# Split buffers two and two, result rows first on ScalarE, and the first gathers one by one: a change to a Fourier-and-experts kernel

## The chip, the cores and the metric

The kernel runs on one core of a Trainium2 chip. The metric is device time in microseconds, the median of several runs; one further execution was profiled.

## The reference, cut to what matters

The input `x` has 8 sequences of 1856 rows of 256 numbers. The reference takes the real part of its two-dimensional Fourier transform, and sends each of the 14,848 rows through one of 16 experts:

```python
X = np.fft.fft(x, axis=1); x = np.fft.fft(X, axis=2).real.reshape(B * S, D)
g_idx = argmax(x @ w_group)            # one of 4 groups
e_idx = argmax(x_g @ w_expert[g])      # one of 4 experts in it
h = maximum(x_e @ w1[g, e], 0)         # 256 -> 1024
ye = h @ w2[g, e]                      # 1024 -> 256
out[tokens] = (g_w * e_w)[:, None] * ye   # two softmax weights
```

## The kernel before, in words

**First phase.** `phase1` computes the transform batch by batch as matmuls in pairs of fp16 halves (a number is a high half plus a low half), chooses an expert for each row, and writes the rows of 260 words with their token number and weight to the DRAM tensor `XS`. The order of its steps is written out by hand, as the letters of `ORDER0` to `ORDER8`. Its last part, `last_rows`, is left over as a "tail" that the second phase runs between its own steps.

**Second phase.** `phase2` works through 44 jobs. A slot is 128 rows of one expert, and a job is one to four slots. The jobs are: 0, 1 and 2, the first four slots of experts 0, 1 and 2, taken before all batches are routed (kind "e"); 3, 4 and 5, three more slots of each (kind "s"); 6 and 7, four and three slots of expert 3; 8, one overflow slot (kind "o", whose expert is read from a table at run time); 9 and 10, expert 4; 11, overflow; and so on to expert 15. Overflow slots take the rows of experts that have more than seven slots.

For each slot POOL gathers 128 rows from `XS` by an indirect DMA (`gather`, L1243) into one of eight `xg` buffers. `turn_steps` casts the high half on ScalarE (L1263) into `xh`, of which there are four, makes the low half on VectorE (L1265), and a transposing DMA on SP's queue (L1271) writes `xT`. `layer1` makes eight groups of six matmuls (`ph`, L1301), each followed by a relu on ScalarE (L1304) and the low half on VectorE (L1305). `layer2` makes 24 matmuls a slot (`py`, L1317), ScalarE scales the result into one of four `y` buffers (L1322), and POOL stores it to `out` with an indirect DMA (L941). PSUM has four banks for `ph` and two for `py`.

**Weights.** A unit is the weights of one expert, 2 MB. `load_weights` (L1189) brings them into a staging buffer `wst`; `split_steps` squares them on ScalarE (`junk`), adds the sums across partitions with a tiny matmul on PE (`pn`, L1211), derives a power of two on VectorE, and writes the high half on ScalarE and the low half on VectorE into a split buffer `whl`. Before the change there is a staging `w` for experts' own weights, one for overflow weights (`wo`), three split buffers for own weights (`wa`, `w2`, `wx`, used in turn) and one for overflow weights (in `wo`). The list `todo` holds the units in the order in which their split buffers come free; `weights` makes one step of the first unit on it when that unit's buffer is free, and starts the next load into the same staging when a split ends. `begun` lets own units beyond the first three wait for job 3 and overflow units for job 4.

**Order.** While job n runs, its iteration starts the gathers of job n+2 (`fetch`, `serve`: all of a job's slots at once), emits `layer1` of job n, `layer2` of job n-1, and between the pieces (`tick`) steps of the weights' split, of the tail, and of the turning of job n+1 (`prep`). A piece of layer 1 counts 320 a slot and a piece of layer 2 counts 2570 of planned time, and a weights step is made for each 800 (1000 during the tail). This is the order in which the program is written down; the framework's scheduler then orders each engine's queue, by that order as priority and by planned times, except where `InOrder` (the names `self.A`, `self.V`, ...) pins an instruction behind those written down before it on its engine. The first two jobs' gathers, casts and transposes are emitted in the first phase, by `first_turn`: all eight gathers, then the casts.

```python
return "w", ("wa", "w2", "wx")[e % 3]     # pools(u): staging, split buffer
```

Of the kernel before, what the change touches and what calls it, by code (L numbers as in the profile page):

```python
# [49 lines left out]
STEADY = 8  # L50

# [252 lines left out]
class K:  # L304
# [780 lines left out]
    def early_load(self, e, r):  # L1085

        b, ii, ge = self.early[e, r]
        return self.gather(self.xp2, ii, b), ge
# [151 lines left out]
    def gather(self, pool, ap, b=None):  # L1240

        xg = pool.tile([P, RWID], F32, name="xg")
        ins = self.nc.gpsimd.indirect_dma_start(  # L1243
            out=xg[:, :].bitcast(I32), out_offset=None, in_=self.XS[:, :],
            in_offset=bass.IndirectOffsetOnAxis(ap=ap, axis=0),
            bounds_check=B * BSTEP, oob_is_err=False).ins
        if b is not None:
            self.of_batch(ins, b)
        return xg

    def turn_steps(self, qp, xgs, ges, V, A, Q, most=4, bufs=(3, 4)):
# [9 lines left out]
        for j, xg in enumerate(xgs):  # L1261
            xh = qp.tile([P, 2, D], F16, name="xh", bufs=bufs[1])
            A.copy(xh[:, 0], xg[:, 0:D])  # L1263
# [14 lines left out]
    def first_turn(self):  # L1278

        jobs = [[(e, r) for r in range(a, z)] for e, a, z in waves()[0][1]]  # L1280
        while jobs[-1][-1] not in self.early:
            yield
        xs = [list(zip(*(self.early_load(*j) for j in job))) for job in jobs]
        yield
        self.x0 = []
        most = max(map(len, jobs))
        for xgs, ges in xs:
            self.x0.append((yield from self.turn_steps(self.xp0, xgs, ges, self.V, self.A, self.Q, most,
                                                       (len(jobs), most))))
# [20 lines left out]
    def layer2(self, qp, w, hT, cws, toks, group="out"):  # L1310
        nc = self.nc
        for j, (cw, tok) in enumerate(zip(cws, toks)):
# [9 lines left out]
            nc.scalar.activation(y, py, AF.Copy, scale=cw)  # L1322
# [17 lines left out]
    def phase2(self, wp):  # L1340
        tc, nc = self.tc, self.nc
        wpa = self.wpa
        with tc.tile_pool(name="h", bufs=2, reuse_waits="tile") as hp, \
# [26 lines left out]
            def pools(u):  # L1370
                kind, e = units[u]
                if kind == "o":
                    return "wo", "wo"
                return "w", ("wa", "w2", "wx")[e % 3]
# [11 lines left out]
            state = dict(split=None, done=-1, t=0, tail=self.last_rows(), job=0)  # L1386
            begun = lambda u: u < len(first) or state["job"] >= LATER + (units[u][0] == "o")

            def tail():
                if state["tail"]:  # L1390
                    try:
                        next(state["tail"])
                    except StopIteration:
                        state["tail"] = None
                        pool["wo"] = later.enter_context(
                            tc.tile_pool(name="wo", bufs=1, side="right", reuse_waits="tile"))
                    serve()
# [13 lines left out]
            def weights():  # L1411

                if state["split"] is None:
                    if not todo or free(todo[0]) > state["done"] or (units[todo[0]][0] == "o" and "o" not in infos) \
                            or not begun(todo[0]):
# [14 lines left out]
            def fetch(n):  # L1430
                if n < len(jobs):
                    want.append(n)
                    serve()

            def serve():
                while want:
                    n = want[0]
                    _, kind, slots = jobs[n]
                    if state["tail"] and (kind != "e" or any(j not in self.early for j in slots)):
                        return  # L1440
                    want.pop(0)
                    if kind == "e":
                        if n >= len(self.x0):
                            xs[n] = list(zip(*(self.early_load(*j) for j in slots)))
# [3 lines left out]
                    if kind == "o" and "o" not in infos:  # L1448
                        infos["o"] = self.overflow_info(pool["wo"])
                    ii, ge = infos[kind]  # L1450
                    xs[n] = ([self.gather(self.xp2, ii[:, j:j + 1]) for j in slots],
                             [ge[:, j:j + 1] for j in slots])

            def prep(n):
                if n < len(jobs):
                    while n in want:
                        tail()
                    xs[n] = self.x0[n] if n < len(self.x0) else \
# [3 lines left out]
            def tick(g, t):  # L1462
                if t == T1 and state["job"] >= STEADY:
# [114 lines left out]
```

## Time and profile before

| | us |
|---|---|
| median of 3 runs | 861.6 |
| runs | 860.82, 861.6, 865.37 |
| profiled execution | 868.83 |
| its span, first to last instruction | 867.0 |

The span has 17,751 instructions. The mean granted TensorE clock over it is 0.991 of full speed. The first phase fills about the first 185 us; the first matmul of the expert layers is at 185.5 us. In the rows below, "busy" is time in which an engine executes, a wait is put down to what released it last, and SPq, POOLq and so on are the queues' own instructions, such as the issue of a DMA. PE is TensorE's matmuls, PEld its weight loads, ACT ScalarE, DVE VectorE, POOL GpSimd.

### The profile page before, as it was taken

To read this page: it belongs to the slowest core of one execution; us is meant where nothing else is said; L and a number is where in the kernel's file an instruction comes from. 1 tells how busy PE (TensorE), PEld (TensorE's weight loads), DVE (VectorE), ACT (ScalarE), POOL (GpSimd) and SP (SyncE) were. 2 spreads that over 40 slices of the span, in tenths; PEclk is the share of its full clock that TensorE was granted. 3 is DMA by queue.
4 is the path that set the end of the run, shared out by engine and by line. 5 is a ranking of instruction groups with operands and counts; after the bars stand their busy time and mean duration, and the time that the engine had idled before them with its cause. 6 is when DMAs were issued, how large, how long until landed. Compare 5 with 4: busy or idle time off the path is not lost. (4 is left out here: it accounts for less than half of the span.)

```text
span 867.0 us, 17751 instructions
## 1 busy us (share of the span) xinstructions
PE 815.2 (94%) x6491; PEld 585.2 (67%) x6491; DVE 550.6 (64%) x1381; ACT 581.1 (67%) x1190; POOL 318.7 (37%) x326
## 2 busy tenths in 40 slices
PE   1899999989889998999999999999999989999996
PEld 0467666656557776686868686868686858686865
DVE  6469998789863755474756566665656556654440
ACT  2477676876645876686777778686868677865531
POOL 1023211413674415253535262526262626240302
PEclk9999999999999999999999999999999999999998
DMA  9677973385686546565657574858485757443201
GB/s 348 192 223 202 248 219 136 141 233 214 143 192 200 161 147 195 127 175 160 177 167 199 132 225 106 218 126 242 94 226 114 225 105 226 119 139 64 63 5 42
DMA packets 105515, 144.53 MB, mean 167 GB/s; under 512 B 75194, under 2 KB 77638, under 8 KB 103888
## 3 DMA queue, kind: packets, MB, share of 16 engines
q1 hardware_dynamic: 91360, 106.15, 41.1%
q0 software_dynamic: 13632, 36.99, 18.2%
q8 instruction: 52, 0.85, 0.4%
q14 instruction: 39, 0.32, 0.1%
q10 hardware_dynamic: 432, 0.22, 0.1%
HBM read 97.41 MB, written 31.72 MB: 149 GB/s over the span
## 5 line engine op out<-in xcount | busy, mean ns | idle before, releaser
L1301 PE MATMUL ph<-xT,whl 128*128 128x512 f16 (+2 forms) x2112 | 353.9, 317 | 7.7 <-DVE hT L1305 5.0
L1317 PE MATMUL py<-whl,hT 128*128 128x256 f16 x2976 | 356.8, 272 | 4.2 <-ACT y L1322 4.2
L1317 PEld LDWEIGHTS <-hT 128*128 128x128 f16 x2976 | 287.2, 98 | 60.5 <-issue 7.6
L1305 DVE SCALAR_TENSOR_TENSOR hT<-ph,hT 128x512 f16<-128x512 f32 (+2 forms) x352 | 178.0, 529 | 156.6 <-ACT hT L1304 152.9
L1301 PEld LDWEIGHTS <-whl 128*128 128x128 f16 x2112 | 184.1, 98 | 128.2 <-issue 8.1
L941 POOL DMA_INDIRECT out<-y,tok x124 | 142.6, 1150 | 262.7 <-ACT y L1322 214.2
L1304 ACT ACTIVATE hT<-ph 128x512 f16<-128x512 f32 (+2 forms) x352 | 156.1, 471 | 50.4 <-PE ph L1301 45.4
L1243 POOL DMA_INDIRECT xg<-XS,ii_s x100 | 116.0, 1160 | 133.3 <-ACT hT L1304 83.8
L282 DVE SCALAR_TENSOR_TENSOR whl<-wst,e_v,whl 128x1024 f16<-128x1024 f32 x112 | 140.0, 1281 | 26.1 <-ACT whl L282 24.8
L282 ACT ACTIVATE whl<-wst,e_v 128x1024 f16<-128x1024 f32 x112 | 123.8, 1139 | 24.1 <-DVE e_v L282 21.4
L282 ACT ACTIVATE junk<-wst 128x1024 bf16<-128x1024 f32 x112 | 118.4, 1057 | 12.2 <-DMA wst<-w 11.8
L1322 ACT ACTIVATE y<-py,cws 128x256 f32<-128x256 f32 x124 | 58.3, 472 | 55.7 <-PE py L1317 39.2
L1263 ACT CAST xh<-xg 128x256 f16<-128x256 f32 x112 | 43.2, 403 | 70.8 <-DMA xT<-xh 64.1
L1265 DVE TENSOR_TENSOR xh<-xg,xh 128x256 f16<-128x256 f32 x112 | 46.6, 419 | 66.4 <-ACT xh L1263 66.3
L282 PE MATMUL pu<-CS,ghl 128*128 128x464 f16 (+3 forms) x384 | 81.9, 364 | 3.5 <-ACT ghl L282 3.5
L282 PEld LDWEIGHTS <-ghl 128*128 128x128 f16 (+1 forms) x384 | 43.7, 118 | 32.8 <-ACT ghl L282 3.5
L282 PEld LDWEIGHTS <-U 128*128 128x128 f16 x672 | 44.4, 99 | 14.4 <-issue 3.5
L282 PE MATMUL pr<-c,U 128*128 128x256 f16 x336 | 48.9, 283 | 3.5 <-DMA U<-un 2.2
L282 ACT CAST U<-pu 128x464 f16<-128x464 f32 (+3 forms) x64 | 32.7, 549 | 17.2 <-PE pu L282 16.2
L282 POOL DMA_DIRECT2D xq<-xq x12 | 11.0, 1072 | 85.4 <-DVE xq L282 26.5
L282 DVE TENSOR_TENSOR xq<-xq 128x514 f32<-128x514 f32 x40 | 25.4, 687 | 6.4 <-DMA xq<-xq 6.4
L282 DVE SCALAR_TENSOR_TENSOR ghl<-BD,x_v,ghl 128x512 f16<-128x512 f32 (+1 forms) x30 | 21.8, 781 | 2.1 <-ACT ghl L282 2.1
(183 smaller groups left out, 462.4 us busy)
## 6 DMA issues: line engine op xcount, KB each, us to landing
wst<-w SPq DMA_DIRECT2D x108, 512.0 KB, 8.2
xq<-xq SPq DMA_DIRECT2D x8, 1028.0 KB
xq<-xq POOLq DMA_DIRECT2D x12, 514.0 KB, 5.7
XS<-whl SPq DMA_DIRECT2D x6, 910.0 KB
CS<-cs SPq DMA_DIRECT2D x8, 464.5 KB, 10.2
XS<-row SPq DMA_DIRECT2D x3, 1040.0 KB
XS<-row SPq DMA_DIRECT2D x3, 910.0 KB
XS<-xq SPq DMA_DIRECT2D x3, 910.0 KB
```

The costliest lines, as they stand in the source:

```text
L282: return self.tc.keep_in_program_order(f(*args, **kw))
L941: ins = self.nc.gpsimd.indirect_dma_start(out=out, out_offset=bass.IndirectOffsetOnAxis(ap=ap, axis=0), in_=in_, in_offset=None, bounds_ch ...
L1243: ins = self.nc.gpsimd.indirect_dma_start(out=xg[:, :].bitcast(I32), out_offset=None, in_=self.XS[:, :], in_offset=bass.IndirectOffsetOnAx ...
L1263: A.copy(xh[:, 0], xg[:, 0:D])
L1265: lo = V.tensor_tensor(out=xh[:, 1], in0=xg[:, 0:D], in1=xh[:, 0], op=ALU.subtract)
L1301: nc.tensor.matmul(ph[:, 0:n * P], lhsT=w[:, wl, o:o + P], rhs=xT[:, xl * 2 + c, :], start=i == 0, stop=i == 5)
L1304: self.relu = nc.scalar.activation(hT[:, f, 0], ph[:, 0:n * P], AF.Relu).ins.name
L1305: nc.vector.scalar_tensor_tensor(out=hT[:, f, 1], in0=ph[:, 0:n * P], scalar=0.0, in1=hT[:, f, 0], op0=ALU.max, op1=ALU.subtract)
L1317: nc.tensor.matmul(py, lhsT=hT[:, f, hl, j * P:(j + 1) * P], rhs=w[:, wl, 2048 + f * D:2048 + (f + 1) * D], start=i == 0, stop=i == 23)
L1322: nc.scalar.activation(y, py, AF.Copy, scale=cw)
```

## The change

It has three parts.

- **Split buffers.** Own weights of the experts from 3 on use two split buffers in turn (`wo`, `w2`), overflow weights two others (`wa`, `wx`). The first three experts keep `wa`, `w2` and `wx`. The staging buffers stay as they were.
- **Result rows.** The activation that scales `py` into `y` is given a priority 400 places ahead of its place.
- **Gathers.** While the job number is under 8, the gathers of job n+2 are handed out one at a time, at every second piece of layer 1 of job n, each with a wait for the relu just emitted. From job 8 on they go out all at once as before. When the tail ends, what is then due goes out at once, behind the last relu emitted. In `first_turn` job 1's gathers come behind the first cast of job 0, with a wait for it.

```diff
--- before.py
+++ after.py
@@ -48,6 +48,7 @@
 LATER = 3
 OVER_AT = 4
 STEADY = 8
+URGENT = 400
 
 RATE, RATE2, T1, T2 = 1000, 800, 320, 2570
 
@@ -1082,10 +1083,10 @@
                                  in1=self.carry[:, e:e + 1].broadcast_to([P, r1 - r0]), op=ALU.is_ge)
         self.V.tensor_tensor(out=self.carry, in0=self.carry, in1=self.c32[:, o:o + NE], op=ALU.max)
 
-    def early_load(self, e, r):
+    def early_load(self, e, r, after=None):
 
         b, ii, ge = self.early[e, r]
-        return self.gather(self.xp2, ii, b), ge
+        return self.gather(self.xp2, ii, b, after), ge
 
     def of_batch(self, ins, b):
 
@@ -1237,7 +1238,7 @@
         self.w0 = yield from self.split_steps(self.wpa, self.st0, self.V, self.A, self.M,
                                               self.misc[:, 488:490])
 
-    def gather(self, pool, ap, b=None):
+    def gather(self, pool, ap, b=None, after=None):
 
         xg = pool.tile([P, RWID], F32, name="xg")
         ins = self.nc.gpsimd.indirect_dma_start(
@@ -1246,7 +1247,14 @@
             bounds_check=B * BSTEP, oob_is_err=False).ins
         if b is not None:
             self.of_batch(ins, b)
+        if after:
+            self.behind(ins, after)
         return xg
+
+    def behind(self, ins, name):
+
+        self.tc.add_manual_dep(ins, name, mybir.DependencyInfo(
+            mybir.DependencyClass.Sync, mybir.DependencyReason.DATA), reason="not before it")
 
     def turn_steps(self, qp, xgs, ges, V, A, Q, most=4, bufs=(3, 4)):
 
@@ -1260,7 +1268,7 @@
         xT = xT[:, :, 0:n * P]
         for j, xg in enumerate(xgs):
             xh = qp.tile([P, 2, D], F16, name="xh", bufs=bufs[1])
-            A.copy(xh[:, 0], xg[:, 0:D])
+            self.cast = A.copy(xh[:, 0], xg[:, 0:D]).ins.name
             yield
             lo = V.tensor_tensor(out=xh[:, 1], in0=xg[:, 0:D], in1=xh[:, 0], op=ALU.subtract)
             tw = V.scalar_tensor_tensor(out=wt[:, j], in0=ges[j].broadcast_to([P, 2]), scalar=BIG,
@@ -1280,13 +1288,18 @@
         jobs = [[(e, r) for r in range(a, z)] for e, a, z in waves()[0][1]]
         while jobs[-1][-1] not in self.early:
             yield
-        xs = [list(zip(*(self.early_load(*j) for j in job))) for job in jobs]
+        load = lambda job, after=None: list(zip(*(self.early_load(*j, after) for j in job)))
+        xs = load(jobs[0])
         yield
         self.x0 = []
         most = max(map(len, jobs))
-        for xgs, ges in xs:
-            self.x0.append((yield from self.turn_steps(self.xp0, xgs, ges, self.V, self.A, self.Q, most,
-                                                       (len(jobs), most))))
+        for i in range(len(jobs)):
+            steps = self.turn_steps(self.xp0, *xs, self.V, self.A, self.Q, most, (len(jobs), most))
+            next(steps)
+            if i + 1 < len(jobs):
+                xs = load(jobs[i + 1], self.cast)
+            yield
+            self.x0.append((yield from steps))
 
     def layer1(self, qp, w, xT, n):
         nc = self.nc
@@ -1319,7 +1332,8 @@
                                      start=i == 0, stop=i == 23)
                     i += 1
             y = qp.tile([P, D], F32, name="y", bufs=4)
-            nc.scalar.activation(y, py, AF.Copy, scale=cw)
+            with self.tc.high_priority(URGENT):
+                nc.scalar.activation(y, py, AF.Copy, scale=cw)
             if group is None:
                 nc.gpsimd.indirect_dma_start(
                     out=self.ap["out"], out_offset=bass.IndirectOffsetOnAxis(ap=tok, axis=0),
@@ -1370,8 +1384,8 @@
             def pools(u):
                 kind, e = units[u]
                 if kind == "o":
-                    return "wo", "wo"
-                return "w", ("wa", "w2", "wx")[e % 3]
+                    return "wo", ("wa", "wx")[e % 2]
+                return "w", ("wa", "w2", "wx")[e] if e < len(first) else ("wo", "w2")[(e - len(first)) % 2]
 
             pool = {"w": wp, "wa": wpa, "w2": wp2, "wx": wpx}
             last, before = {}, {}
@@ -1383,7 +1397,7 @@
             todo = sorted(range(1, len(units)), key=lambda u: (max(free(u), 0), u))
             st, ready, infos, xs, want = {}, {0: self.w0}, {}, {}, []
             self.scratch = wpx.tile([P, 2, 4096], F16, name="whl").rearrange("p h n -> p (h n)")
-            state = dict(split=None, done=-1, t=0, tail=self.last_rows(), job=0)
+            state = dict(split=None, done=-1, t=0, tail=self.last_rows(), job=0, turn=False)
             begun = lambda u: u < len(first) or state["job"] >= LATER + (units[u][0] == "o")
 
             def tail():
@@ -1394,7 +1408,7 @@
                         state["tail"] = None
                         pool["wo"] = later.enter_context(
                             tc.tile_pool(name="wo", bufs=1, side="right", reuse_waits="tile"))
-                    serve()
+                    serve(len(want))
 
             def load(u):
                 kind, e = units[u]
@@ -1412,7 +1426,7 @@
 
                 if state["split"] is None:
                     if not todo or free(todo[0]) > state["done"] or (units[todo[0]][0] == "o" and "o" not in infos) \
-                            or not begun(todo[0]):
+                            or not begun(todo[0]) or pools(todo[0])[1] not in pool:
                         return False
                     loads()
                     pn = self.ps.tile([P, 2], F32, name="pn", tag="r" if state["tail"] else "misc")
@@ -1428,38 +1442,45 @@
                 return True
 
             def fetch(n):
-                if n < len(jobs):
-                    want.append(n)
-                    serve()
-
-            def serve():
-                while want:
-                    n = want[0]
-                    _, kind, slots = jobs[n]
-                    if state["tail"] and (kind != "e" or any(j not in self.early for j in slots)):
+                if len(self.x0) <= n < len(jobs):
+                    xs[n] = []
+                    want.extend((n, j) for j in jobs[n][2])
+                    if state["job"] >= STEADY:
+                        serve(len(want))
+
+            def serve(most):
+                while want and most:
+                    n, j = want[0]
+                    kind = jobs[n][1]
+                    if state["tail"] and (kind != "e" or any(i not in self.early for i in jobs[n][2])):
                         return
                     want.pop(0)
+                    most -= 1
                     if kind == "e":
-                        if n >= len(self.x0):
-                            xs[n] = list(zip(*(self.early_load(*j) for j in slots)))
+                        xs[n].append(self.early_load(*j))
                         continue
                     if not infos:
                         infos["s"] = self.static_info()
                     if kind == "o" and "o" not in infos:
                         infos["o"] = self.overflow_info(pool["wo"])
                     ii, ge = infos[kind]
-                    xs[n] = ([self.gather(self.xp2, ii[:, j:j + 1]) for j in slots],
-                             [ge[:, j:j + 1] for j in slots])
+                    xs[n].append((self.gather(self.xp2, ii[:, j:j + 1], after=self.relu if state["job"] < STEADY else None), ge[:, j:j + 1]))
 
             def prep(n):
                 if n < len(jobs):
-                    while n in want:
+                    while any(i == n for i, _ in want):
                         tail()
+                        serve(1)
+                    if n in xs:
+                        xs[n] = list(zip(*xs[n]))
                     xs[n] = self.x0[n] if n < len(self.x0) else \
                         (yield from self.turn_steps(qp, *xs[n], *((self.V, self.A) if jobs[n][1] == "e" else
                                                                   (nc.vector, nc.scalar)), nc.sync))
 
             def tick(g, t):
+                state["turn"] ^= t != T2
+                if state["turn"]:
+                    serve(1)
                 if t == T1 and state["job"] >= STEADY:
                     return next(g, None)
                 state["t"] += t
```

## Rows read from the trace of the kernel before

**Rows 1.** The page's busy time, share of the span and instructions.

```profile
PE 815.2 (94%) x6491; PEld 585.2 (67%) x6491; DVE 550.6 (64%) x1381; ACT 581.1 (67%) x1190; POOL 318.7 (37%) x326
```

**Rows 2.** The chain that ended last: start us, us, what.

```profile
734.94 1.75 PE py L1317 x16
736.69 5.18 PE ph L1301 x24
...
775.50 1.34 PE ph L1301 x24
```

**Rows 3.** PE's waits from 180 us on: us in total, times, longest.

```profile
PE ph L1301 <- DVE hT L1305: 5.0, 3, 2.5
PE py L1317 <- ACT y L1322: 4.2, 5, 1.4
PE ph L1301 <- ACT xh L1263: 2.7, 1, 2.7
PE pn L1211 <- ACT junk L282: 2.2, 2, 1.9
```

**Rows 4.** Two stretches: us, busy of PE, PEld, DVE, ACT, POOL; clock, DMA share, GB/s.

```profile
230.00:243.00 13.00, 12.92 (x70) 7.29 (x70) 11.04 (x26) 4.82 (x12) 10.86 (x8) 0.87 0.92 164
243.00:256.00 13.00, 10.61 (x71) 6.84 (x70) 8.36 (x25) 5.55 (x14) 9.96 (x10) 1.00 1.06 245
```

**Rows 5.** Timeline around 340 us: start, us, engine, instruction [idle before it].

```profile
336.72 4.27 ACT L282 ACTIVATE whl<-wst,e_v 128x1024 f16<-128x1024 f32 x4 [0.27 <-DVE e_v L282]
...
341.49 0.83 ACT L1322 ACTIVATE y<-py,cws 128x256 f32<-128x256 f32 x2
342.01 3.22 PE L1317 MATMUL py<-whl,hT 128*128 128x256 f16 x28 [1.45 <-ACT y L1322]
```

**Rows 6.** The page's groups: busy us, mean ns of one, idle before.

```profile
L282 ACT ACTIVATE whl<-wst,e_v 128x1024 f16<-128x1024 f32 x112 | 123.8, 1139 | 24.1 <-DVE e_v L282 21.4
L282 ACT ACTIVATE junk<-wst 128x1024 bf16<-128x1024 f32 x112 | 118.4, 1057 | 12.2 <-DMA wst<-w 11.8
...
L1263 ACT CAST xh<-xg 128x256 f16<-128x256 f32 x112 | 43.2, 403 | 70.8 <-DMA xT<-xh 64.1
```

**Rows 7.** Timeline around 327 us, a weight split that waits for its load.

```profile
322.76 1.80 SPq L1189 DMA_DIRECT2D wst<-w  x4
...
326.77 1.06 ACT L282 ACTIVATE junk<-wst 128x1024 bf16<-128x1024 f32 x1 [2.37 <-DMA wst<-w]
...
332.41 0.16 PE L1211 MATMUL pn<-wacc,one_b 128*128 128x2 bf16 x1 [1.89 <-ACT junk L282]
```

**Rows 8.** Timeline of POOL, of SP's queue and of PE, 224 to 266 us.

```profile
224.81 1.12 POOL L1243 DMA_INDIRECT xg<-XS,ii_s  x1 [0.50 <-DVE wst L1118]
...
236.80 1.00 POOL L1243 DMA_INDIRECT xg<-XS,ii_s  x1 [0.30 <-issue]
...
243.61 22.12 SPq L1271 DMA_TRANSPOSE xT<-xh  x9
...
256.16 2.11 PE L1301 MATMUL ph<-xT,whl 128*128 128x384 f16 x12 [2.54 <-DVE hT L1305]
```

**Rows 9.** ScalarE's waits from 184 to 350 us.

```profile
ACT xh L1263 <- DMA xT<-xh: 16.2, 10, 3.5
```

**Rows 10.** Line 1243, the gathers: ns min/median/max, and us from issue to landing.

```profile
L1243 POOL DMA_INDIRECT xg<-XS,ii_s x100: 994/1032/2073, 224.8 to 761.8; - x100
...
DMA to landing us min/median/max: 2.8/6.2/10.3
```

**Rows 11.** Line 1271, the transposes from 236 to 350 us.

```profile
L1271 SPq DMA_TRANSPOSE xT<-xh x23: 1189/1215/3878, 235.4 to 347.6; - x23
...
DMA to landing us min/median/max: 2.5/6.9/8.0
```

**Rows 12.** Timeline at the first job: SP's queue and PE.

```profile
172.09 7.33 SPq L282 DMA_TRANSPOSE xT<-xh  x4
...
185.48 2.32 PE L1301 MATMUL ph<-xT,whl 128*128 128x512 f16 x10
```

## The prediction

> **What bounds the kernel now.** I began with the page's busy times: PE is busy for 815.2 us, 94% of the span [rows 1]. That alone does not say that PE is the bound, so I read the chain of waits next. In the steady part 24 matmuls of 512 columns take 5.18 us, 24 of 128 columns 1.34 us and 16 of 256 columns 1.75 us, that is 216, 56 and 109 ns each [rows 2]; 512 columns at 2.4 GHz are 213 ns, so while PE runs it runs at its rate. The change takes no matmul away. All it can win is time in which PE stands or has the lower clock.
>
> So the list of who waited for whom, for PE alone and from 180 us on (the expert layers), is the list of what can be won [rows 3]: 5.0 us for VectorE's halves of hT, 4.2 us for result rows (y) that ScalarE has not yet taken out of PSUM, 2.7 us on the ScalarE casts of xh, and 2.2 us for the squares of a weight split: 14.1 us in all, 1.6% of the time (smaller ones left out). The stretch from 230 to 243 us has a mean granted clock of 0.87 [rows 4], after PE had stood 2.7 us before 230: 13% of 13 us is 1.7 us more. The ceiling is thus about 16 us, a time of 846. 0.5% of 861.6 us, what a measurement of this kernel can tell from no change, is 4.3 us: I need more than a quarter of the ceiling for a gain that counts.
>
> **The change, part by part.** The durations are of the profiled execution: 868.8 us, span 867.0, so 1.8 us lie around the span. The median of the runs is 861.6, that is 7.2 us below it. I take the sum off the median unscaled; if profiling itself lengthened waits, it is a little too large.
>
> *Result rows first.* The change adds nothing here: the same 124 activations stand earlier in ScalarE's order. Around 342 us the row shows what that is worth: ScalarE does four weight casts in a row from 336.72 to 340.99, and the two y come only from 341.49 on; PE, which has only two PSUM banks for py, resumes at 342.01 after 1.45 us [rows 5]. A y put between two weight casts would have been early enough. There are five such waits with 4.2 us [rows 3]. If the order is obeyed they go, but a y can still come behind one cast of 1.14 us [rows 6] that has begun. Bounds 0 and 4.2; I take 3.6, nearer to the upper end, as PE's rows around 342 us show a bank waiting through four casts and not through one. What y passes (relus, casts) is 0.42 us later each time (0.83 for two [rows 5]); 4 PSUM banks of ph cover a relu. Without that cover it would be 0.42 us a result row, 52 us over 124 of them; the row nearest to that is VectorE's 5.0 us, so I charge it under new waits below.
>
> *Split buffers.* Before, own weights have three buffers and overflow weights one; and the first steps go overflow 0, expert 3, expert 4, expert 5. The last three share one staging buffer, so each load can start only when the split before it has finished: the load issued at 322.76 is awaited by the squares at 326.77 (2.37 us), and PE's tiny matmul on their sums stands 1.89 us behind them [rows 7]; that is the longer of the two waits that make up the 2.2 us [rows 3]. After, the order is expert 3, overflow 0, expert 4, overflow 1, expert 5: the two stagings alternate, so a load has a whole split to land in (ScalarE's part alone is 4 x 1.06 + 4 x 1.14 = 8.8 us [rows 6]). I take all 2.2; 0 at the other end, if the wait goes on to another load. In the steady part, an overflow weight need no longer be split between two neighbouring overflow jobs; the trace books no PE wait to that, so 0, at most the 2.7 us of the largest wait [rows 3]. For the own weights the cover gets thinner: two buffers in place of three. A cycle of seven own slots and one overflow slot is 8 x 6 x (216 + 162) ns + 7 x 24 x 109 ns + 48 x 56 ns + 24 x 109 ns = 41.7 us of PE [rows 2], with 162 as 3/4 of 216; two splits of 19 steps at one step per 0.8 us of planned PE time are 30.4 us. 11 us are left, so 0.
>
> *Gathers one by one.* The number stays; 21 gathers (of jobs 3 to 9) get a wait for a relu, 4 (of job 1) for a cast. Before, POOL runs eight row gathers of jobs 3 to 5 from 224.81 to 237.80 in one go [rows 8], and more as buffers come free; DMA is full from 243 to 256 us (share 1.06) [rows 4]; nine transposes take from 243.61 to 265.73 to issue [rows 8]; ScalarE's xh casts wait for xh buffers that transposes still read (16.2 us in ten waits from 184 to 350) [rows 9], the relus behind them in its queue are late, and PE stands 2.54 us before 256.16 [rows 8]. With the gathers of job n+2 spread over the first layer of job n, later casts can't stand ahead of those relus. Bounds: 0 (weight loads and result stores crowd the same stretch, and expert 3's split now falls into it) and 2.5; I take 1.3, the middle, as nothing in the trace shows that stretch without gathers.
>
> The DMA transfers of all queues do share: a stretch that is full is full for everyone. The Trainium skill, DMA: Bandwidth & Descriptors (Issuing engines are not separate DMA queues), says that transfers begun by any engine interleave on the same 16 DMA engines. The share of 1.06 agrees; taken strictly, moving the gathers would give back all 2.5, and the sum below would be 1.2 us lower.
>
> What is queued behind a waiting gather: POOL's result stores, on which the four y buffers hang. And the chain from a gather to its job: 1.03 us issue, 6.2 landing, 0.4 cast [rows 6, 10], 0.4 on VectorE (taken like the cast), 1.2 + 6.9 transpose [rows 11]: 16.1 us. The last gather of a job goes out at the seventh of eight relus; until job n+2 starts PE still has, for three-slot jobs, about 1 us of that layer, 7.9 of a second layer (72 x 109 ns) and 15.7 of the next job: 24.6 us. 8.5 us of margin, so 0 in the sum. If that cover were gone, a job would start late: the price is with the rivals.
>
> *First two jobs.* Job 1's four gathers move behind job 0's first cast. They then share DMA with job 0's four transposes (issued from 172.09 to 179.42), whose result PE needs at 185.48 [rows 12]. Bounds: 1 us earlier (job 0's own gathers are alone, one gather's 1.03 us [rows 10]) to 4.1 us later (four gathers in front of the transposes); I take 0, as 6 us lie between the last issue and the need.
>
> *New waits.* A new order on ScalarE and POOL makes some of its own. I charge 1.0 us, a fifth of VectorE's 5.0 [rows 3]; bounds 0 and 5.0.
>
> Sum: -3.6 - 2.2 - 1.3 + 1.0 = -6.1 us, 861.6 to 855.5.
>
> **Rivals.** *The waits move on* (no change). The steady jobs still get their gathers in one go, and the 2.5 of the 5.0 us behind VectorE that lie outside the gap at 256 stay. If splits and gathers only shift their crowding and half of y-first is lost to later relus, 1.8 us remain: 859.8. For it: the change shortens no transfer, so ScalarE's 16.2 us of waiting [rows 9] may only be spread otherwise. Against it: the y waits have one plain cause.
>
> *It reaches further.* If the spread gathers also free the transposes before 230, the 2.7 us there and the 1.7 us of lower clock go too, and gathers count in full: 6.1 + 4.4 + 1.2 = 11.7, a time of 849.9. Against it: job 3's gathers, the first of the eight, are handed out when the first phase's tail ends, as before, behind a relu of job 1 that is then over; they stay where they are.
>
> *The gate holds up the jobs* (slower). A gather at the head of POOL's queue waits for its relu, the stores behind it wait too, rows arrive late, and jobs 4 to 9 begin without xT. The price is that of the one job that the trace shows late, 2.7 us at 230 [rows 3]: six jobs are 16.3 us, less the 6.1, a time of 871.8; the sign turns from the third late job on (8.1 against 6.1). It decides when the chain of 16.1 us exceeds the 24.6. For it: gathers have landed in up to 10.3 us [rows 10]. Against it: the margin. The Trainium skill, DMA: Bandwidth & Descriptors (SWDGE vs HWDGE vs iDMA), states that the software path has a single queue allocated, so that stores cannot pass a gather. The trace agrees in so far as POOL's gathers run one at a time [rows 8]; it does not show a store held up by one.
>
> *It doesn't do what it says*: the order on ScalarE is made from a plan of times; if the plan never has a y and another instruction ready together, y-first changes nothing, and 2.5 us remain: 859.1. I count this with the first rival.
>
> **How the numbers follow.** Forecast 0.52, waits move 0.24, further 0.15, slower 0.09. Faster by over 0.5% means under 857.3: about 0.7 of the forecast's chance (its own range is 850 to 861: y-first and new waits at either end), all of "further", a fifth of "waits move": 0.56. Slower (over 865.9): most of the gate and a little of new waits, 0.09. The rest, 0.35. The range takes in "further" with 1.4 us more and "waits move" with about 4 us of new waits: 848.5 to 863.5.
>
> **What would show it.** Right: PE's waits for y near 0 with y directly after its py; no PE wait on squares between 320 and 335, where no load is awaited; POOL's gathers between 230 and 260 apart from each other, PE without a gap near 256. Wrong: PE waits for xT or weights at job starts between 240 and 360; VectorE's 5.0 us grown; PE idle from 180 us on above 12 us.

## The result, and the profile after

The changed kernel takes 872.22 us, the median of four runs (871.77 to 877.94), beside 862.22 us of the kernel before in the same comparison. The ratio is 1.0126, 95% interval 1.0088 to 1.0164: slower by 1.3%, 10 us. The forecast was 855.5 with a range to 863.5. The profiled execution took 872.49 us, with a span of 870.7.

First the list of what PE waited for from 180 us on, as in [rows 3] (total us, times, longest):

```profile
PE ph L1314 <- DVE hT L1318: 7.4, 5, 4.2
PE ph L1314 <- DMA xT<-xh: 3.0, 1, 3.0
PE py L1330 <- ACT y L1336: 2.5, 5, 1.0
PE pn L1212 <- ACT junk L283: 1.8, 3, 1.4
```

That is 14.7 us, no more than the 14.1 us of [rows 3], and yet the kernel is 10 us slower. So one of the two profiles does not stand for its kernel. The kernel before was profiled once more, on a chip where its median is 860.5 us; that execution took 860.31 us (the one of [rows 3] took 868.83), the shortest of its four (860.31 to 864.55), and its list is:

```profile
PE ph L1301 <- DMA xT<-xh: 2.4, 1, 2.4
PE pn L1211 <- ACT junk L282: 1.9, 1, 1.9
PE py L1317 <- ACT y L1322: 1.6, 3, 0.6
PE ph L1301 <- DVE hT L1305: 0.6, 2, 0.4
```

6.5 us. More than half of the waits that the prediction set out to win are not there in an execution that took the usual time. A second profile at the usual time, that of e2_yfirst below (860.50 us), sums to 6.5 us as well. The profile of 860.31 us is "the repeat" from here on, and after is read against it.

Against the repeat, PE stands 8.2 us longer from 180 us on. The windows of after show the clock too (busy time and instructions of each engine, then granted clock, DMA share, GB/s):

```profile
230.00:243.00 13.00, 12.93 (x59) 6.43 (x59) 5.32 (x14) 3.87 (x9) 6.18 (x5) 0.77 0.88 230
243.00:256.00 13.00, 13.00 (x89) 8.55 (x88) 6.68 (x18) 9.27 (x20) 4.05 (x4) 1.00 0.33 80
340.00:372.00 32.00, 27.65 (x207) 18.79 (x205) 14.56 (x46) 17.01 (x41) 20.77 (x20) 0.95 0.73 176
```

The aim was reached: from 243 to 256 us the DMA share is 0.33, where it was 1.06 [rows 4], and PE has no gap at 256. But PE stands 3.0 us before 230, where it stood 2.7 [rows 3] and in the repeat 2.4, and the clock falls behind it; and a new hole lies between 340 and 372. The clock is at its lower level (half, 1.2 GHz) for 6.83 us from 229.17 and 3.41 us from 362.29, while in the repeat it stays at the upper one from 185.27 to 854.28. The fall near 230 is not the change's own: it is in the first profile of the kernel before (0.87 from 230 to 243 us [rows 4]) and in that of e2_yfirst (also 0.87). At half the rate that is worth up to half of 10.24, 5.1 us. 8.2 + 5.1, less the 2.3 us by which the first expert matmul comes earlier (185.00 against 187.33), is 11.0 of the 12.2 us between the two spans (870.7, 858.5). Where the time goes can be read from the start of each job's first layer, in us:

| first layer of job | 0 | 2 | 7 | 9 | 10 | 12 |
|---|---|---|---|---|---|---|
| the repeat | 187.33 | 231.07 | 315.53 | 347.51 | 360.55 | 389.42 |
| after | 185.00 | 230.07 | 317.80 | 352.07 | 371.06 | 399.93 |
| after is later by | -2.3 | -1.0 | 2.3 | 4.6 | 10.5 | 10.5 |

About half of it, 5.9 us, is lost within job 9, where the hole and the second fall of the clock lie; what is left is spread over the jobs before it and the last 1.7 us behind job 12.

What is late on ScalarE, from 225 to 372 us, in after:

```profile
ACT y L1336 <- DMA out<-y,tok: 10.5, 2, 6.6
ACT xh L1271 <- DMA xg<-XS,ii_s: 8.9, 4, 2.9
ACT xh L1271 <- DMA xg<-XS,ii_o: 3.4, 1, 3.4
ACT xh L1271 <- DMA xT<-xh: 2.3, 3, 1.3
```

Before, the casts waited for transposes (16.2 us) [rows 9]; now they wait for the gathers, 12.3 us, and hardly for transposes. All idle time ahead of casts is 21.4 us here and 20.9 in the repeat: it has changed its cause, not its size. What is new is the first line, a result row that waits for a store. The timeline of ScalarE around it, then PE's, then POOL's:

```profile
338.73 0.46 ACT L1336 ACTIVATE y<-py,cws 128x256 f32<-128x256 f32 x1
...
356.64 0.47 ACT L1336 ACTIVATE y<-py,cws 128x256 f32<-128x256 f32 x1 [6.56 <-DMA out<-y,tok]
...
361.16 0.59 ACT L1317 ACTIVATE hT<-ph 128x512 f16<-128x512 f32 x1
```

```profile
362.53 1.86 PE L1314 MATMUL ph<-xT,whl 128*128 128x512 f16 x4 [4.24 <-DVE hT L1318]
```

```profile
346.86 1.02 POOL L942 DMA_INDIRECT out<-y,tok  x1 [0.31 <-issue]
...
350.83 1.02 POOL L1244 DMA_INDIRECT xg<-XS,ii_s  x1 [0.30 <-DVE hT L1318]
352.16 1.02 POOL L942 DMA_INDIRECT out<-y,tok  x1 [0.30 <-issue]
353.48 1.02 POOL L1244 DMA_INDIRECT xg<-XS,ii_s  x1 [0.30 <-issue]
354.81 1.00 POOL L1244 DMA_INDIRECT xg<-XS,ii_s  x1 [0.31 <-issue]
356.12 1.00 POOL L1244 DMA_INDIRECT xg<-XS,ii_o  x1 [0.30 <-issue]
357.42 1.03 POOL L942 DMA_INDIRECT out<-y,tok  x1 [0.30 <-ACT xh L1271]
```

At job 8 the handing out one by one ends, and POOL catches up with the gathers held back: from 334 to 367 us its timeline shows seventeen gathers (the last of job 9 to those of job 15) and seven stores without a pause longer than 0.31 us. Each store stands in the queue behind gathers, and the four y buffers stay occupied. The row of 338.73 is ready at 339.19; its store goes out at 346.86, 7.7 us later, and takes 9.7 us to land. The y at 356.64, four results on, waits 6.56 us for that buffer. The relu behind it on ScalarE comes at 361.16, after four casts, which stand another 2.3 us on transposes, and a second y; PE resumes at 362.53 after 4.24 us, with the lower clock. In the repeat the same seventeen gathers are spread over 261 to 354 us, because POOL had run 21 gathers between 226 and 262. The Trainium skill, DMA: Bandwidth & Descriptors (SWDGE vs HWDGE vs iDMA), states that the software path has one queue allocated. That a store cannot pass a gather is a step from it, which these rows bear out: gathers and stores leave POOL one at a time, 1.0 us each, and here a store is seen held up behind gathers.

### The profile page after: what moved, and what is told of

Its sections match the earlier page's. It is cut to its first block, busy times and chain, and to the rows that moved or that the text cites. A ratio compares the mean times of both kernels' runs of the same rounds, so it can differ in the third digit from the quotient of the medians.

```text
span 870.7 us, 17750 instructions
## 1 busy us (share of the span) xinstructions
PE 816.3 (94%) x6491; PEld 584.5 (67%) x6491; DVE 551.2 (63%) x1381; ACT 580.3 (67%) x1190; POOL 319.0 (37%) x326
## 4 chain that ended last, share of the span: by engine, by line
PE 43%; DMA 16%; DVE 11%; issue 10%; ACT 7%; POOL 3%; SPq 0%; POOLq 0%; ACTq 0%; DVEq 0%
PE py L1330 21%; PE ph L1314 20%; DMA xT<-xh 11%; ACT junk L283 3%; DMA wst<-w 2%; POOL out L942 2%; ACT hT L1317 2%; ACT whl L283 1%; DVE ghl L283 1%; DVE xq L283 1%; DVE hT L1318 1%; POOL xg L1244 1%; DVE xT L283 1%; PE pu L283 1%; PE pr L283 1%
## 5 line engine op out<-in xcount | busy, mean ns | idle before, releaser
L1314 PE MATMUL ph<-xT,whl 128*128 128x512 f16 (+2 forms) x2112 | 358.0, 318 | 10.4 <-DVE hT L1318 7.4
L1318 DVE SCALAR_TENSOR_TENSOR hT<-ph,hT 128x512 f16<-128x512 f32 (+2 forms) x352 | 180.9, 530 | 161.3 <-ACT hT L1317 159.7
L1314 PEld LDWEIGHTS <-whl 128*128 128x128 f16 x2112 | 183.7, 98 | 134.1 <-issue 16.9
L942 POOL DMA_INDIRECT out<-y,tok x124 | 145.5, 1173 | 255.4 <-ACT y L1336 208.6
L1244 POOL DMA_INDIRECT xg<-XS,ii_s x100 | 111.7, 1116 | 145.9 <-ACT hT L1317 107.2
L283 PE MATMUL pr<-c,U 128*128 128x256 f16 x336 | 47.1, 276 | 3.1 <-DMA U<-un 2.2
L1244 POOL DMA_INDIRECT xg<-XS,ii_e x12 | 14.2, 1184 | 25.2 <-DVE ghl L283 12.4
```

The costliest lines, as they stand in the source:

```text
L283: return self.tc.keep_in_program_order(f(*args, **kw))
L942: ins = self.nc.gpsimd.indirect_dma_start(out=out, out_offset=bass.IndirectOffsetOnAxis(ap=ap, axis=0), in_=in_, in_offset=None, bounds_ch ...
L1244: ins = self.nc.gpsimd.indirect_dma_start(out=xg[:, :].bitcast(I32), out_offset=None, in_=self.XS[:, :], in_offset=bass.IndirectOffsetOnAx ...
L1314: nc.tensor.matmul(ph[:, 0:n * P], lhsT=w[:, wl, o:o + P], rhs=xT[:, xl * 2 + c, :], start=i == 0, stop=i == 5)
L1318: nc.vector.scalar_tensor_tensor(out=hT[:, f, 1], in0=ph[:, 0:n * P], scalar=0.0, in1=hT[:, f, 0], op0=ALU.max, op1=ALU.subtract)
```

## The experiments

Five chips came into it, by the numbers that the record gives them. On chip 2, where e0 to e3 ran, the kernel before takes 860.5 us. On chips 1 (e4 to e7), 15 (f), 4 (g) and 3 (h) it takes 878.4, 879.7, 879.5 and 880.0; these four are "the other chips" below. The chip of the result above is not recorded; its 862.2 us for the kernel before is near chip 2's. Ratios are to the kernel before on the same chip; they are the record's, and not quotients of the medians shown (863.7 by 860.5 would be 1.004). The runs on chip 2:

| run | kernel | median us | ratio (interval) |
|---|---|---|---|
| e0_before | kernel before, as a control | 863.7 | 1.0054 (1.0033 to 1.0075) |
| e1_split | split buffers alone | 863.63 | 1.0056 (1.0033 to 1.0079) |
| e2_yfirst | y first alone | 860.32 | 1.0007 (0.9983 to 1.0032) |
| e3_gather | the gathers' part alone, first jobs too | 870.09 | 1.0132 (1.0098 to 1.0167) |

> The kernel before, once more, for a second profile: the profiled execution of before (868.8 us) lies 7 us above its median (862.2). All theories: the time is 862 within 3 us. If the profile of an execution near 862 lacks most of the PE gaps read there (14.1 us of waits), the gains forecast had little to win; if it has the same gaps, they stand.

> Split buffers two and two alone. Theory hand-over (the loss of the changed kernel sits where the gathers go from one by one to all at once, around job 8, and needs the gathers part): within 3 us of before, -2 to +1. Theory own buffers (two instead of three make own splits late): +5 to +10, with PE waits on whl. Theory y-first (a y that waits for a store blocks the relus behind it): within 2 us of before.

> Result rows first alone. Theory hand-over: -3 to 0 us, PE's waits for y under 1.5 us. Theory y-first: +4 to +10 us, with ScalarE's y waiting on out stores and PE on hT after that. Theory own buffers: -3 to 0.

> Gathers one by one alone. Theory hand-over: +3 to +8 us, a run of more than 12 gathers on POOL with few pauses between 325 and 370 us and a PE gap of over 2 us near it. Theory y-first: within 2 us of before, since no y is put ahead. Theory own buffers: -2 to +1.

The control has four runs and comes out 0.5% off itself: a ratio of so few runs, that of the result too, carries half a per cent that its interval does not. So split buffers and y first are worth nothing that can be told, each alone, and the gathers' part is the whole loss within that half per cent. With y first alone PE's waits for y are 1.7 us in three; in the repeat 1.6 in three: nothing was there to win. In e3_gather, ScalarE's list from 225 to 372 us has the same two signs as after:

```profile
ACT xh L1271 <- DMA xg<-XS,ii_s: 16.4, 8, 4.0
...
ACT y L1335 <- DMA out<-y,tok: 8.1, 1, 8.1
```

**The other chips: taking the gathers' part apart.**

```diff
 e4_paced_all (the changed kernel, and:)
-                    if state["job"] >= STEADY:
-                        serve(len(want))
-  ... after=self.relu if state["job"] < STEADY else None)
+  ... after=self.relu)
 e5_no_relu_wait, g2_no_relu_wait
-  ... after=self.relu if state["job"] < STEADY else None)
+  ... )
 e6_y8
-            y = qp.tile([P, D], F32, name="y", bufs=4)
+            y = qp.tile([P, D], F32, name="y", bufs=8)
 e7_first_only, f3_first_again (of the gathers' part only first_turn's; no split buffers, no y first)
 f4_first_y (the same and y first)
 f1_lag8, g3_lag8
+            self.past = getattr(self, "past", []) + [relu]
+            self.past_relu = self.past[-9] if len(self.past) >= 9 else None
-  ... after=self.relu if state["job"] < STEADY else None)
+  ... after=self.past_relu if state["job"] < STEADY else None)
 f2_no_gather (split buffers and y first; the gathers as before)
 g4_no_first (the changed kernel, with first_turn as before)
 h2_paced_lag8 (e4_paced_all, with after=self.past_relu)
```

| run | median us | ratio (interval) |
|---|---|---|
| e4_paced_all | 915.9 | 1.045 (1.043 to 1.0471) |
| e5_no_relu_wait | 875.8 | 0.997 (0.9944 to 0.9995) |
| e6_y8 | 882.75 | 1.0067 (1.0042 to 1.0093) |
| e7_first_only | 874.17 | 0.9954 (0.9921 to 0.9987) |
| f1_lag8 | 878.53 | 0.9989 (0.9964 to 1.0014) |
| f2_no_gather | 882.91 | 1.003 (1.0002 to 1.0058) |
| f3_first_again | 873.11 | 0.9922 (0.9893 to 0.9951) |
| f4_first_y | 874.18 | 0.9932 (0.9899 to 0.9964) |
| g1_after | 877.97 | 0.9986 (0.9956 to 1.0017) |
| g2_no_relu_wait | 875.31 | 0.9973 (0.9942 to 1.0005) |
| g3_lag8 | 877.39 | 0.9969 (0.9941 to 0.9997) |
| g4_no_first | 885.4 | 1.0062 (1.0034 to 1.0089) |
| h1_before | 878.96 | 0.9993 (0.9961 to 1.0025) |
| h2_paced_lag8 | 906.24 | 1.0312 (1.0262 to 1.0361) |

> The changed kernel with the gathers handed out one by one behind relus in all jobs, so that there is no passage from one by one to all at once at job 8. Theory hand-over (18 gathers catch up on POOL from 334 to 366 us, result stores stand behind them, four y buffers run out, ScalarE's y waits for a store): no run of gathers there, no y wait of over 3 us on a store, 862 to 866. Theory lost lead (one-by-one gathers arrive only just before their casts, ScalarE's queue waits on them): as slow as the changed kernel or slower, 872 to 885, with casts waiting on gathers all along.

Handing out all gathers one by one costs 4.5%. So the passage to at-once at job 8 is not the only thing that costs: without it it gets worse. ScalarE's first line from 380 to 830 us, and two of POOL's:

```profile
ACT xh L1271 <- DMA xg<-XS,ii_s: 113.0, 44, 6.3
```

```profile
POOL out L942 <- ACT y L1336: 158.7, 51, 10.7
POOL xg L1244 <- ACT hT L1317: 60.3, 32, 4.2
```

Casts wait 113 us for gathers (in the repeat there is no such line in this stretch), and what stands behind them on ScalarE is late: from 180 us on PE waits 19.0 us for squares and 14.2 for halves of hT. POOL's two lines do not set this kernel apart: in the repeat, whose gathers run ahead, the same lines are 148.6 and 76.1 us. The order of its queue gives an example of how a gather comes late: the store at 462.68 us has waited 10.72 us for its y; the gather behind it goes at 465.13, with its own wait for a relu, and a cast stands until 469.80 for it. A gather handed out one by one has a store before it in the queue that cannot go before the running job has a result.

> The changed kernel with the gathers still handed out one by one, but without their wait for a relu. Theory lost lead: the gathers run ahead again as far as the eight xg buffers allow, casts no longer wait on gathers, 860 to 865. Theory hand-over: if the burst comes from the order in which the gathers are handed out, it stays and so does most of the loss, 868 to 873. Theory first turn (the loss is from job 1's gathers behind the first cast): 870 to 873.

> The changed kernel with eight y buffers instead of four, so that a y need not wait for the store of four results earlier. Theory hand-over: the y waits on stores go (10.5 us of ScalarE waiting between 225 and 372 us), and with them the 4.2 us gap and 1.7 us of clock at 362 us: 864 to 868. Theory lost lead: the gap at 362 us shrinks, but the losses from 283 to 323 us stay: 866 to 870.

> Of the gathers part only that of the first two jobs (job 1's gathers behind the first cast); otherwise the kernel before. Theories hand-over and lost lead: within 3 us of before. Theory first turn: +6 us or more.

With the wait taken out the gathers run ahead again and the ratio is below 1; with eight y buffers it is about half as far above 1 as in the result; the first jobs' part alone is a small gain. Read beside the 1.0126 of the result, this looked like a proof. It was not, since the changed kernel itself had not been timed on this chip (chip 1).

> The changed kernel, whole, with its wait kept: each gather of the first eight jobs waits for a relu, but for the one eight relus (about one job) further back than in the changed kernel. Theory 'lost lead' (the gathers come so late that ScalarE's casts wait for their landing): a lead of a job is back, the casts no longer wait for the gathers, the loss is gone, ratio 0.995 to 1.003. Rival 'the wait itself' (a wait on a relu costs POOL or ScalarE something wherever that relu stands): the loss stays, ratio 1.009 to 1.016. In between (1.004 to 1.008) part of the loss is in the hand-over at job 8 or in too few buffers of the gathered rows.

> The change without its gathers: split buffers two and two, and y first on ScalarE; the gathers as in the kernel before. If the gathers are the whole of the loss and the two other parts are worth nothing together as they were each alone: ratio 0.997 to 1.004. If the two parts help only together, as the forecast had it (3.6 + 2.2 us): ratio 0.992 to 0.994. If they carry a part of the loss: over 1.006.

> Of the whole change only this: the second job's first rows are fetched behind the first job's first cast. A second measurement of the kernel that gave 0.9954. If that was a real gain: again 0.993 to 0.998. If it was the scatter of a few runs, as the repeated kernel before showed (1.0054): 0.998 to 1.004.

> The second job's first rows behind the first job's first cast, and y first on ScalarE; buffers and the other gathers as in the kernel before. If y first is worth nothing, as alone (1.0007): the same ratio as the kernel with the first of the two only, within 0.003. If it helps once the first turns are early: lower by 0.004 or more, 0.988 to 0.992.

The small gain of the first jobs' part came again, and y first adds nothing to it (0.9932 beside 0.9922). Split and y first together cost 0.3%: they do not help together either. The wait put a job back gives 0.9989, as "lost lead" said.

> The changed kernel as it is, beside its variants on one chip. Theory 'lost lead': slower than the kernel before on whichever chip, 1.008 to 1.016, and by 0.008 or more above the two variants of this call without the late wait. Rival 'the chip': on the chip with the slower kernel before, no loss, 0.996 to 1.003, level with the two variants.

> The changed kernel without the wait on the relu; the gathers still handed out one by one. Lost lead: 0.993 to 1.001, at least 0.008 below the changed kernel of this call. The chip: level with it within 0.004.

> The changed kernel with each wait put eight relus (about a job) further back. Lost lead: 0.996 to 1.003, at least 0.008 below the changed kernel of this call. The chip, or the wait itself: level with the changed kernel within 0.004.

> The changed kernel without its first turns' part (job 1's rows fetched at once, as before). As that part alone gave 0.9954 and 0.9922: above the changed kernel of this call by 0.004 to 0.008. If the gain of that part was swallowed by the late gathers: level with it within 0.003.

Here the rival "the chip" won: on chip 4 the changed kernel loses nothing, 0.9986, and its variants without the late wait lie only 0.0013 and 0.0017 lower, within each other's intervals. The runs e5, f1, g2 and g3 therefore don't show that the wait is the price. Nor does e6: with eight y buffers it is at 1.0067 on chip 1, above the changed kernel's 0.9986 on chip 4, and no run says why. g4_no_first, 0.8% slower than g1_after, shows that on this chip the first jobs' part is worth that much to the changed kernel.

> The kernel before, profiled, as a control. If it runs at about 879 us: theory 'two prices' (on this chip dense runs of gathers and stores on POOL bring stalls of TensorE and ScalarE, and late gathers cost as much as the stalls that spreading saves) expects one or two stalls of 3 to 11 us of both engines, with no releaser, between 235 and 310 us, behind the dense runs of gathers from 226 us on. The rival (the chip is slower everywhere) expects no such stall, and the 18 us spread over the span. If it runs at about 861 us: no such stall, ratio 0.998 to 1.005.

> The changed kernel with the gathers of all jobs handed out one by one, each behind a relu eight relus (about a job) further back, no passage to at-once. The same kernel without that lead gave 1.045. Lost lead: with the lead back 1.000 or less; where dense runs bring stalls (before at 879 us) no stall and 0.98 to 0.99; where they don't (861 us) 0.997 to 1.003. If the handing out itself, not the lead, costs: 1.02 to 1.045.

**Why the other chips hide the loss.** On chip 3 the profile of the kernel before (h1) has two stretches in which PE runs one matmul in each 0.7 or 1.4 us, waiting for nothing that the profile shows. The first lies ahead of the expert layers, the second in job 3's first layer:

```profile
169.32 0.49 PE L282 MATMUL pr<-c,U 128*128 128x256 f16 x3 [0.91 <-issue]
169.64 0.18 PE L282 MATMUL look<-RW,U 128*128 128x40 f16 x1
170.07 0.18 PE L282 MATMUL look<-RW,U 128*128 128x40 f16 x1 [0.25 <-issue]
170.79 0.18 PE L282 MATMUL look<-RW,U 128*128 128x40 f16 x1 [0.54 <-issue]
171.53 0.18 PE L282 MATMUL look<-RW,U 128*128 128x40 f16 x1 [0.55 <-issue]
...
259.84 0.32 PE L1301 MATMUL ph<-xT,whl 128*128 128x384 f16 x1 [1.18 <-issue]
261.30 0.32 PE L1301 MATMUL ph<-xT,whl 128*128 128x384 f16 x1 [1.13 <-issue]
262.02 0.32 PE L1301 MATMUL ph<-xT,whl 128*128 128x384 f16 x1 [0.40 <-issue]
```

ScalarE stands with it, 7.01 us before 172.32, put down to "remote". The first falls at the end of the eight gathers of the first two jobs (issued from 160.13 to 169.99), the second behind the run of gathers from 233 to 261. After has four gathers there, then four from 171.8, and this is how the first matmul of the expert layers stands in the profiles:

| | eight gathers in one go | four and four |
|---|---|---|
| the result's runs and chip 2 | 185.48 (before), 187.33 (e0), 186.42 (e1), 187.05 (e2) | 185.00 (after), 185.75 (e3) |
| chip 1 | | 186.17 (e4), 185.04 (e5), 187.63 (e6), 186.85 (e7) |
| chip 15 | 194.65 (f2) | 187.92 (f1), 185.70 (f3), 186.71 (f4) |
| chip 4 | 191.81 (g4) | 186.99 (g1), 187.22 (g2), 187.22 (g3) |
| chip 3 | 193.85 (h1) | 186.69 (h2) |

Compared on one chip, splitting that run is worth 5 to 9 us at this point on chips 15, 4 and 3; on chip 2, nothing to 2. All twelve profiles of kernels with dense runs of gathers and stores on the other chips have such stretches, of 4 to 12 us of PE's waits "issue" in all, most of it in the last part of a run or just behind it; the two without dense runs (e4, h2) have 0.5 and 0.3 us. The profiles of chip 2 and of the result have none, though dense runs stand in them too, so a dense run alone does not bring a stall. In g1_after it lies in the run at job 8:

```profile
345.96 0.22 PE L1314 MATMUL ph<-xT,whl 128*128 128x128 f16 x1 [1.90 <-issue]
346.70 0.22 PE L1314 MATMUL ph<-xT,whl 128*128 128x128 f16 x1 [0.53 <-issue]
347.41 0.23 PE L1314 MATMUL ph<-xT,whl 128*128 128x128 f16 x1 [0.49 <-issue]
```

```profile
354.71 0.47 ACT L1336 ACTIVATE y<-py,cws 128x256 f32<-128x256 f32 x1 [9.66 <-remote]
```

So on these chips the kernel before has its stalls ahead of job 0 and in job 3 (h1, 8.5 us of "issue" in all), and the changed kernel has its own at job 8 (g1, 7.4 us) and gains at job 0; on chip 4 the two take 879.5 and 878.0 us. That its late gathers cost anything there is not shown. What holds up PE and ScalarE behind a dense run, and why not on chip 2, no run here shows.

In h2_paced_lag8 the relu waited for lies a job back, but only 1.4 of the 4.5% came back (h2 on chip 3, e4 on chip 1). Its lines from 380 to 830 us:

```profile
ACT xh L1271 <- DMA xg<-XS,ii_o: 63.4, 10, 7.5
ACT xh L1271 <- DMA xg<-XS,ii_s: 48.0, 36, 4.0
```

```profile
POOL out L942 <- ACT y L1339: 158.3, 50, 6.5
POOL xg L1244 <- ACT hT L1317: 39.8, 34, 3.1
POOL xg L1244 <- DVE wt L1274: 35.7, 10, 4.5
```

The waits for relus fell from 60.3 to 39.8 us, but the gathers now also stand 35.7 us for a step on VectorE that reads an earlier row (L1274), a line that e4 doesn't have: 75.5 us in all. The stores' waits for y stayed at 158 and the casts wait as long as before (111.4 us, 113.0 in e4). So putting the semaphore a job back did not bring the lead back. Which of the three then makes the gathers late (the stores ahead of them, the relu, an earlier row still in use), these runs don't separate. That handing out one by one does not do it by itself, without a wait, e5 and g2 show for the first jobs: there eight gathers run in one go from 224 us, as before. (f1_lag8 and g3_lag8 restored no lead either: between 225 and 372 us f1's casts waited 17.7 us for gathers and g3's 16.9, where the changed kernel's, in g1, waited 15.2.)

## Why the prediction was wrong

**The step that failed** is "8.5 us of margin, so 0 in the sum", with the gain of 1.3 us beside it. The gathers' part alone is 1.0132 on chip 2: about 10 us slower (870.1 beside 860.5), where the prediction had 1.3 us faster. The margin counted the chain from a relu to the job as if a gather left when its relu is done. It had named what stands around the gathers on POOL, the result stores, but had priced them at nothing. The chain of 16.1 us itself was not taken too short: in the repeat gathers land in 2.9 us and transposes in 3.4 (medians), where it had 6.2 and 6.9. From 225 to 372 us POOL stands 37.7 us at stores that wait for y and 25.1 at gathers that wait for relus (in the repeat 47.4 and 4.0, with the gathers that matter already out); what it has put off it makes up for in one run, and there the y buffers hang on it. That the late gathers cause the loss is read from the traces of after and e3, which have casts that wait for gathers and a y that waits for a store, where the repeat has neither, and from e4, where more of it costs more; it is not shown by a run that removes them where the loss is. Taking the wait out was tried on the other chips only, and on chip 4, the one of these on which the changed kernel was timed, there was no loss to cure. Of the 12.2 us between after and the repeat, 5.9 are lost within job 9, at the end of that run of gathers; e3 takes 18.4 us for the same job where the repeat takes 13.0 (352.96 to 371.32, 347.51 to 360.55). What the rest is made of stays open in part.

**The ceiling** of 16 us came from one execution that was 7.2 us above the median. The prediction noted that distance, but costed the waits as if all executions had them. The repeat has 6.5 us of waits and no lower clock between 185 and 854 us: a ceiling of 6.5 us, 0.8%, of which the sum of 6.1 would have been nearly all.

**Result rows first**, -3.6: alone 1.0007, nothing. Its waits were 4.2 us in [rows 3] and 1.6 in the repeat; the bound of 0 was right. With a y placed first, a wait of y for its buffer also holds up ScalarE's relus (356.64 above), which the prediction didn't count; but e3 has such a wait too, 8.1 us, without y first.

**Split buffers**, -2.2: alone 1.0056, level with the control's 1.0054. PE's waits on squares are 1.8 us in after, 1.9 in the repeat: they moved from 332 to other places (296.42, 1.41 us).

**The gap at 256** went, as forecast, and DMA was freed there. It was 2.5 us in the profile read and 0.38 in the repeat.

**First two jobs**, 0: right where the loss is, as far as it shows (the first expert matmul at 185.00); on the other chips worth 0.5 to 0.8%, for a reason that no row of before held.

**The rivals.** "The gate holds up the jobs" came to 871.8 us, and 872.2 were measured, but not by its mechanism: jobs did not begin without xT (PE waits for xT once, 3.0 us; the repeat 2.4). That the two times agree is luck. Stores held up behind gathers, named in this rival, do occur, through the y buffers. Of the prediction's signs of being wrong two came: VectorE's 5.0 us grew to 7.4, and PE stands 14.7 us from 180 us on, above 12. The rival's chance of 0.09 was too small: the change takes away a lead that cost nothing in the repeat, and only a profile with the gap at 256 made that look like a gain.

**A better version.** The first jobs' part alone beats the kernel before on chips 1 and 15: 0.9954 and 0.9922. The whole change is at 0.9986 on chip 4; the two were not timed on one chip, and the first jobs' part alone was not timed on chip 2.

## What to carry to other kernels

Before costing waits of a microsecond, see whether the profiled execution took the median time; one that is 7 us above it showed twice the waits of two that took the usual time. A gather that runs far ahead is a reserve: a wait before it costs not only until the semaphore comes, but moves it in its engine's queue behind everything that waits for the running job, and what is held back comes in one run later. And a variant belongs on the same chip as the change it takes apart: e5, e6 and f1 seemed to cure, in whole or in part, a loss that the change itself had not been shown to have on their chips.

## What was not expected of the hardware

One and the same kernel takes 860.5 us on chip 2 and 878.4 to 880.0 on chips 1, 3, 4 and 15, 2% more. The record doesn't show what sets them apart: each chip was used in one stretch of runs only, so the chip and the time of the runs can't be told from each other. The difference is not even: of the 20.8 us between the profiles of e0 and h1, 6.5 are there at job 0 (187.33, 193.85), and from there on PE waits 9.8 us longer (6.5, 16.3); in kernels without dense runs of gathers (e4, h2) PE has almost none of the stalls. By the ratio the change is 1.3% slower in the result and level on chip 4.
